# Gated mix of two attentions on one core: where the single maximum matmul stands around a step that has none

## The chip, the core and the metric

The kernel runs on one core of one Trainium2 chip. The metric is the device time of one execution in microseconds (us); lower is better. Before the change the median of three runs is 1461.88 us (1461.84 to 1462.23). A profiled execution is one more run, with the hardware profiler on.

The engines of the core have short names in the profile: PE is TensorE (matmuls; PEld is its weight loads), DVE is VectorE, ACT is ScalarE, POOL is GpSimd, SP issues DMAs.

## The reference

```python
x = A_x                                                     # (1, 2048, 512)
g = _sigmoid((x * gate_w).sum(-1, keepdims=True))
a = _A_ref(x, A_wqkv, A_wo)          # 32 heads of 16, window of 8 keys, 2 apart
b = _B_ref(x, B_wq, B_wk, B_wv, B_wo)
return g * a + (1 - g) * b

def _B_ref(x, wq, wk, wv, wo):       # 32 query heads of 16, one key/value head
    q = (x @ wq).reshape(B, S, H, Dh).transpose(0, 2, 1, 3)
    k, v = x @ wk, x @ wv
    scores = jnp.einsum("bhqd,bkd->bhqk", q, k) * (Dh ** -0.5)
    o = jnp.einsum("bhqk,bkd->bhqd", _softmax(scores, axis=-1), v)
    return o.transpose(0, 2, 1, 3).reshape(B, S, H * Dh) @ wo
```

Branch b is most of the work. Each of its 32 heads has 2048 x 2048 scores. Its softmax subtracts the true maximum of each row, so the scores are formed twice: once for the maxima, once for the exponentials.

## The kernel before

**Units and steps.** Branch b is cut into NU = 32 units: 4 blocks of 512 queries by 8 groups of 4 heads. A unit has NJ = 16 steps, one for each tile of 128 keys. There are thus 512 steps, numbered s; `u, kt = divmod(s, NJ)` gives the unit and the step in it. "Second step" below means kt = 1. Units count from 0.

**One step** is laid out by the loop at L1266. For TensorE it holds, in this order:
- the first scores (`exp_pair(s, 0)`, L575): two matmuls into the bank pair `e0` for two heads, in the two halves of the array's rows, followed on ACT by one exp of 128 x 1024 (L577);
- a pair (`fill_pair`, L388 into `pm`): two matmuls of scores for the maxima of a later unit, followed on DVE by a maximum over both (L417);
- perhaps a *single* (`fill_one`, L388 into `ps`, the bank `m1`): one such matmul, and on DVE one maximum (L428);
- the second scores (`exp_pair(s, 1)`, L575), into `e1`, with their exp;
- the weighted group (`weighted(s - 1)`, L585): the exps of the step before times the values, four matmuls into `po`.

The profile calls the banks `e0` and `e1` both `pe`. Scores may go into such a bank only when the exp of the step before has read it. After the last weighted group of a unit (in the first step of the next one) `finish_a` has DVE transpose `po` (L599); the next weighted group, in the second step, overwrites `po` and waits for that.

A step without a single is called *bare* here. The single can go out ahead of the second scores or behind them; the entry "later" at L1309 to L1312 picks the order.

**The planner.** The program that emits the kernel keeps running clocks `clk` of PE, ACT and DVE in us, and in `free` when it thinks that a bank is free. It decides with them what it emits; the chip itself waits on semaphores, not on these clocks. `single_share` (L988) adds to a stock `share`, every step, the singles still to do over the steps still to go, at most 1 a step and 2 in all. `singles` (L979) decides whether step s takes one and takes 1 from the stock. It needs a stock of 1.0, of 0.5 in the last step of a unit, or of 0.3 after a bare step (`bare[0]`). It also refuses when DVE's clock is over `BEHIND` = 1.35 ahead of PE's, unless the last step was bare or the stock is full. `fill_ready` (L1004) then emits the single only if the bank is thought free within M1S = 0.3 us of PE's clock. How many singles there are in all is what the pairs, one a step, leave over (`most`).

The first step of a unit takes none, except in the last eight units (L1316: `kt or not s or u >= NU - 8`).

**Output phases.** In the second steps of units 17 and 25 the loop first calls `out_phase`, which writes 8 and 4 rows of output blocks; that step then runs in the order first scores, single, second scores into `pm`.

Of the kernel before, what the change touches and what calls it, by code (L numbers as in the profile page):

```python
# [18 lines left out]
NJ = S // P  # L19
# [23 lines left out]
BEHIND = 1.35  # L43
FRONT = 468
LEAD, M2S, M1S, E1S, PER_ROW = 3.0, 0.5, 0.3, 0.2, 21
# [36 lines left out]
def gated_mix_kernel(ctx, tc, xt, wa, wk, wq, wo_a, wo_b, out):  # L82
# [21 lines left out]
    def home(v):  # L104

        return (v % NB, v - NB) if v < 2 * NB - 2 else ((v - NB) % (NB - 2), v - NB + 2)
# [3 lines left out]
    m1 = pp.tile([P, 512], F32, name="ps")  # L110
# [7 lines left out]
    clk = {"pe": 0.0, "act": 0.0, "dve": 0.0}  # L118
# [231 lines left out]
    def stack(u):  # L350
        qb, hg = divmod(u, NHG)
        for b in range(2):
            hi, lo = (qd[s, :, qb, 4 * hg + 2 * b:4 * hg + 2 * b + 2, :].rearrange("d c n -> d (c n)") for s in range(2))
            ap = [list(x) for x in hi.ap]
            twice = bass.AP(tensor=hi.tensor, offset=hi.offset, ap=[ap[0], [0, 2]] + ap[1:])
            dst = qst[home(u)[0]].rearrange("p c n -> p (c n)").bitcast(F32)
            nc.sync.dma_start(dst[64 * b:64 * b + 32], twice)
            nc.sync.dma_start(dst[64 * b + 32:64 * b + 48], lo)
        stacked.append(clk["pe"] + (7.5 if pe else 5.0))
# [7 lines left out]
    free = {"m2": 0.0, "m1": 0.0, "e0": 0.0, "e1": 0.0, "po": 0.0}  # L367
# [22 lines left out]
    def to_go():  # L390
        return 2 * len(slots) + len(half)
# [82 lines left out]
    def half_back():  # L474

        nc.sync.dma_start(q67.rearrange("p g x n -> p (g x n)").bitcast(F32), kd.rearrange("p g x n -> p (g x n)"))
        kcd[0] = q67
# [90 lines left out]
    pe, pexp, exped = [], {}, {}  # L568
# [174 lines left out]
    def prepare(j, n, copy=None):  # L743
        nonlocal pool
        hi, lo = turned[j, 1] = [pe[0].tile([P, C, P], F32R, name=f"own{x}", bufs=1) for x in range(2)]
        own = ob[j // 4][:, :n, j % 4 * P:(j % 4 + 1) * P]
        if copy:
            copy(hi[:, :n], own)
            at = max(clk["pe"], pool / 1e3) + 1.3
        else:  # L750
            nc.scalar.activation(hi[:, :n], own, AF.Copy)
            at = after("act", clk["pe"], 0.6)
        nc.gpsimd.tensor_sub(lo[:, :n], own, hi[:, :n].bitcast(F32))
        pool = max(pool, 1e3 * at) + 1300
# [25 lines left out]
    def blocks_out(j):  # L780

        own = p2[0].tile([P, D], F32, name="raw", bufs=1)
        for k in range(2):
            nc.vector.transpose(own[:, k * D // 2:(k + 1) * D // 2], oa[k][:, j, :])
        after("dve", 0, 0.9)
        tasks.append((clk["dve"] + 0.3, blocks_in, (j, own)))
# [180 lines left out]
    def spread_some(k):  # L967

        while (k > 0 or row_left[0] == 1) and later_rows and spread_at[0] <= clk["pe"]:
            x = next(later_rows[0], None)  # L970
            if x is None:
                later_rows.clear()
            else:
                spread_at[0] = clk["pe"] + x
                k -= 1
# [3 lines left out]
    def singles(s):  # L979

        most = to_go() - 2 * max(0, 16 * (NU - 1) - 16 - s) - PER_ROW * max(0, NJ - 4 - outs)
        need = 0.3 if bare[0] else 0.5 if (s + 1) % NJ == 0 else 1.0
        if most <= 0 or share[0] < need or not bare[0] and share[0] < 2.0 and clk["dve"] - clk["pe"] > BEHIND:
            return False
        share[0] -= 1.0
        return True

    def single_share(s):  # L988

        left = 16 * (NU - 1) - 16 - s  # L990
        if left > 0:
            most = to_go() - 2 * left - PER_ROW * max(0, NJ - 4 - outs)
            rate = most / left
            if len(stacked) < NU:
                ready = len(half) + 2 * sum(x[0] < len(stacked) for x in slots[:16 * NB])
                wait = 16 * (home(len(stacked))[1] + 1) + LAND - s
                rate = min(rate, ready / wait - 2)
            share[0] = min(2.0, share[0] + max(0.0, min(1.0, rate)))
        else:
            share[0] = 1.0  # L1000

    share, bare = [0.0], [False]

    def fill_ready(key, slack):  # L1004
        if fillable() and free[key] <= clk["pe"] + slack:
            clk["pe"] = max(clk["pe"], free[key])
            if key == "m1":
                fill_one()
            elif half and (not slots or slots[0][0] >= len(stacked) or stacked[slots[0][0]] > clk["pe"]):
                fill_one(m2[:, 0, :], "m2")  # L1010
            elif slots:
                fill_pair(m2, "m2")

    def pause(most):
        n = 0
        while n < most and slots and fillable():
            key = min(("e0", "e1", "m2"), key=lambda k: free[k])
            clk["pe"] = max(clk["pe"], free[key])
            if half:
                fill_one({"e0": eb[0], "e1": eb[1], "m2": m2}[key][:, 0, :], key)  # L1020
                n += 1
                continue
            fill_pair({"e0": eb[0], "e1": eb[1], "m2": m2}[key], key)
            n += 2
        return n
# [28 lines left out]
    def run_tasks():  # L1054
        for task in [t for t in tasks if t[0] <= clk["pe"]]:
            tasks.remove(task)
            task[1](*task[2])
# [208 lines left out]
    for s in range(NS + 1):  # L1266
        u, kt = divmod(s, NJ)
        if s == 16 * NB + 4:
            half_back()
        if len(stacked) < NU and s >= 16 * (home(len(stacked))[1] + 1):  # L1270
            stack(len(stacked))
        if s < NS and kt == 0 and u not in shifted:
            while u not in shifted:
                clk["pe"] += 0.5
                run_tasks()
                if u not in shifted and left.get(u, 1):
                    assert pause(4)
        v = min(x[0][0] for x in (half, slots, [(NU,)]) if x)
        need = left.get(v, NF // NU)
        steps = 16 * v - 6 - s  # L1280
        short = need - 2.8 * max(0, steps) if v < NU else 0
        lead = (NF - to_go()) / 64 - s / 16
        order = (0, "m2", "later") if s else ()
        rows = 4 if outs else 8
        k, n = (outs + rows) // 4 - 1, C - (outs >= NJ - 4)
        if outs == NJ - 4:
            if s in (16 * NU - 40, 16 * NU - 32):
                blocks_out(outs + (s - 16 * NU + 40) // 8)
            if to_go() <= 9 and not later_rows and "last" not in done:
                later_rows.append(spread(list(range(outs, NJ)), n))  # L1290
            if short > 0 and steps < 2:
                pause(short)
        elif due or outs < NJ and s and kt == 0 and outs // NH in done and NHG * (k + 1) - 1 in shaped and (lead < LEAD or s >= 16 * (NHG * (k + 2) + 1)):
            if not due:
                prepare(outs, n)
                due.append(n)
            else:
                out_phase(list(range(outs, outs + rows)), due.pop(), kt == 1)
                outs += rows
                order = (0, "m1", 2)  # L1300
        elif short > 0 and steps < 2:
            pause(short)

        first = 0
        some = min(4, -(-(row_prods[0] - TO_END) // (NS + 1 - s)))
        order = list(order)
        single_share(s)
        while order:
            which = order.pop(0)  # L1309
            if which == "later":  # L1310
                order = ["m1", 1] if free["e1"] > clk["pe"] - E1S else [1, "m1"]
                first = 0  # L1312
            elif which == "m2":
                fill_ready("m2", M2S)
            elif which == "m1":
                one = not later_rows and (kt or not s or u >= NU - 8) and singles(s)  # L1316
                bare[0] = not one
                if one:
                    first = half[0][4] if half else 0
                    fill_ready("m1", M1S)  # L1320
            elif s < NS:
                if which == 1:
                    spread_some(some)
                exp_pair(s, which % 2 or which // 2, which == 2, first)
        if s == NS:
            spread_some(some)
        if s:
            weighted(s - 1)
            if kt == 0 and s < NS:
                finish_a(u - 1, nc.gpsimd)  # L1330
        run_tasks()
        run_pool()
# [65 lines left out]
```

## Time and profile before

| | |
|---|---|
| median of three runs | 1461.88 us |
| the profiled execution, its own time | 1461.75 us |
| its span, first to last instruction | 1460.0 us |
| mean granted TensorE clock | 0.999 |
| projections and first maxima, until the first exp | 0 to 262.86 us |
| steps 0 to 272 | to 830.2 us |
| output phase in unit 17 | to 904.1 us |
| units 17 to 24 | to 1171.5 us |
| output phase in unit 25 | to 1210.0 us |
| units 25 to 31 | to 1448.2 us |
| the last rows | to 1460.0 us |

How to read the rows. A timeline row has the start in us, the duration in us, the engine, the line, the operation, what it writes and reads, and a count of merged instructions; in brackets stands how long the engine was idle just before, and what ended that wait. A merged row's duration covers all of its instructions. A row of the windows view has start and end of the stretch, its length, then the busy time of PE, PEld, DVE, ACT and POOL in it with the number of instructions, the granted clock, and the DMA engines' share and GB/s. Its sum row adds the lengths. A group row of the page has the shape, the count, the busy time in all, the mean of one in ns, and the engine's idle time before them with what ended it.

### The profile page before, as it was taken

The numbers are of one execution on the slowest core, as the hardware profiler recorded it, in microseconds if no ns is written. First come the engines' busy times: TensorE is split into PE (matmuls) and PEld (weight loads), VectorE is DVE, ScalarE is ACT, GpSimd is POOL, SyncE is SP. The second block draws the span as 40 slices with busy tenths as digits, with TensorE's granted clock in tenths as the row PEclk, the third lists the DMA queues.
The fourth block names the chain that finished last, engine by engine and source line by source line (L and its number), as shares of the span: only waits on it lengthen the run. The fifth ranks groups of instructions, "written<-read, shape, count | busy, mean of one in ns | idle before, by whom it ended". The sixth has DMA issues, their size and how long they took to land.

```text
span 1460.0 us, 28999 instructions
## 1 busy us (share of the span) xinstructions
PE 1450.1 (99%) x10612; PEld 674.5 (46%) x10612; DVE 1192.3 (82%) x1866; ACT 1285.6 (88%) x1627; POOL 1001.5 (69%) x1753
## 2 busy tenths in 40 slices
PE   9999999999999999999999999999999999999998
PEld 5877777433333333333333476333333363333343
DVE  6988889688888888888888888888888888888712
ACT  5659889999999999999999888999999988999986
POOL 7852889878898988988979898788888240011221
PEclk9999999999999999999999999999999999999999
DMA  6752533222021120211211111121120000000110
GB/s 226 210 165 75 148 96 101 70 57 82 27 86 42 45 90 12 72 42 42 74 46 46 60 42 62 40 71 42 42 72 12 12 27 16 12 1 2 29 32 29
DMA packets 75263, 89.80 MB, mean 62 GB/s; under 512 B 56368, under 2 KB 56416, under 8 KB 70896
## 3 DMA queue, kind: packets, MB, share of 16 engines
q1 hardware_dynamic: 68176, 49.00, 12.0%
q0 software_dynamic: 6368, 37.90, 7.8%
q8 instruction: 83, 1.36, 0.4%
q10 hardware_dynamic: 576, 1.05, 0.2%
q14 instruction: 60, 0.49, 0.1%
HBM read 60.03 MB, written 27.35 MB: 60 GB/s over the span
## 4 chain that ended last, share of the span: by engine, by line
PE 96%; DVE 2%; ACT 0%; POOL 0%; issue 0%; DVEq 0%; POOLq 0%; ACTq 0%
PE po L585 35%; PE pe L575 23%; PE pe L1213 11%; PE pm L388 8%; PE ps L388 6%; PE pe L869 4%; PE pm L484 3%; PE ps L484 2%; PE po L484 1%; PE pm L940 1%; PE pe L212 1%; DVE mx L417 1%; DVE mx L428 0%; PE po L186 0%; DVE tt L599 0%
## 5 line engine op out<-in xcount | busy, mean ns | idle before, releaser
L577 ACT ACTIVATE pexp<-pe 128x1024 f32<-128x1024 f32 x1022 | 987.1, 1022 | 83.1 <-PE pe L575 79.9
L417 DVE TENSOR_REDUCE mx<-pm 128x2 f32<-128x1024 f32 x505 | 618.0, 1224 | 144.6 <-PE pm L388 141.1
L585 PE MATMUL po<-pexp,vst 128*32 128x512 f32 x4096 | 545.5, 605 | 0.8 <-DVE tt L599 0.8
L575 PE MATMUL pe<-qst,kst 64*128 64x512 f32 x1916 | 442.2, 451 | 0.0
L575 PEld LDWEIGHTS pe<-qst,kst 64*128 64x128 f32 x1916 | 179.9, 183 | 473.5 <-ACT pexp L577 467.5
L428 DVE TENSOR_REDUCE mx<-ps 128x1 f32<-128x512 f32 x404 | 275.0, 681 | 1.9 <-PE ps L388 1.9
L388 PE MATMUL pm<-kst,qst 62*128 62x512 f32 x975 | 196.8, 397 | 0.4 <-ACT pexp L577 0.4
L649 POOL TENSOR_TENSOR pr<-aext 128x256 f32<-128x256 f32 x256 | 182.0, 738 | 2.8 <-DMA aext<-ad 2.5
L709 POOL TENSOR_TENSOR oa<-oa,av 128x256 f32<-128x256 f32 x224 | 164.1, 732 | 15.0
L585 PEld LDWEIGHTS po<-pexp,vst 128*32 128x32 f32 x4096 | 80.6, 108 | 167.6 <-issue 158.0
L388 PE MATMUL ps<-kst,qst 62*128 62x512 f32 x396 | 156.0, 394 | 0.2 <-DVE mx L428 0.2
L706 POOL TENSOR_TENSOR av<-aext,lg 128x256 f32<-128x256 f32 x224 | 139.3, 622 | 13.5
L1213 PE MATMUL pe<-wah,xh 64*128 64x512 f32 x376 | 119.3, 396 | 1.1 <-DVE stage L318 1.1
L1213 PE MATMUL pe<-wah,xl 64*128 64x512 f32 x376 | 119.7, 394 | 0.0
L1213 PE MATMUL pe<-wal,xh 64*128 64x512 f32 x376 | 118.9, 394 | 0.0
L513 ACT ACTIVATE dd<-pm 128x512 f32<-128x512 f32 x180 | 102.1, 606 | 15.2 <-PE pm L484 6.8
L388 PEld LDWEIGHTS pm<-kst,qst 62*128 62x128 f32 x975 | 94.3, 186 | 4.2 <-DVE mx L417 1.1
L655 POOL TENSOR_TENSOR tr<-pr 128x512 f32<-128x512 f32 x64 | 81.8, 1277 | 4.2
L513 ACT ACTIVATE pexp<-pm 128x512 f32<-128x512 f32 x124 | 70.5, 605 | 14.4 <-PE pm L484 7.0
L655 POOL TENSOR_TENSOR tr<-tr 128x256 f32<-128x256 f32 (+1 forms) x128 | 72.4, 566 | 8.7
L612 POOL TENSOR_TENSOR rl<-rl,gate_t 128x16 f32<-128x16 f32 x31 | 6.9, 221 | 103.6 <-DVE rl L606 96.2
L388 PEld LDWEIGHTS ps<-kst,qst 62*128 62x128 f32 x396 | 74.0, 187 | 4.3 <-issue 1.2
(215 smaller groups left out, 1965.6 us busy)
## 6 DMA issues: line engine op xcount, KB each, us to landing
aext<-ad POOLq DMA_DIRECT2D x32, 1056.0 KB, 5.5
qst<-qd SPq DMA_DIRECT2D x60, 128.0 KB
ad<-stage SPq DMA_DIRECT2D x32, 240.0 KB
xraw<-xt SPq DMA_DIRECT2D x16, 256.0 KB
qd<-qhi SPq DMA_DIRECT2D x16, 256.0 KB
qd<-qlo SPq DMA_DIRECT2D x16, 256.0 KB
qst<-qd SPq DMA_DIRECT2D x60, 64.0 KB
qst<-ml SPq DMA_DIRECT2D x216, 2.0 KB
```

The costliest lines, as they stand in the source:

```text
L388: nc.tensor.matmul(dst, qst[home(v)[0]][b:b + 62, pr, t * P:(t + 1) * P], kst[b:b + 62, kc * 512:(kc + 1) * 512], start=True, stop=True)
L417: nc.vector.tensor_reduce(m[:, :, pr, t, kc], dst, AX.X, ALU.max)
L428: nc.vector.tensor_reduce(m[:, odd, pr, t, kc:kc + 1], dst, AX.X, ALU.max)
L513: nc.scalar.activation(d[:, odd], m2[:, odd, :], AF.Abs)
L575: nc.tensor.matmul(bank[:, odd, :], kst[b:b + 64, kt * P:(kt + 1) * P], qst[home(u)[0]][b:b + 64, pr, :], start=True, stop=True)
L577: nc.scalar.activation(e, bank, AF.Exp, scale=SCALE)
L585: nc.tensor.matmul(po[32 * i:32 * i + 32, :], vst[:, kt, :], pexp[s, i // 2][:, i % 2, :], start=(kt == 0), stop=(kt == NJ - 1))
L649: nc.gpsimd.tensor_mul(pr[:, k], q, e[:, o:o + NH, AC:2 * AC])
L655: nc.gpsimd.tensor_add(nx, cur[:, :, 0:n], cur[:, :, n:2 * n])
L706: nc.gpsimd.tensor_mul(av, e[:, o:o + NH, 2 * AC:].rearrange("p j (h d) -> p j h d", d=DH), lg[:, w].unsqueeze(3).to_broadcast([P, NH, AG, ...
L709: nc.gpsimd.tensor_add(ao, ao, av)
L1213: nc.tensor.matmul(front[2 if x == last else x % 2][0][:, b, :], l[h], r[h], start=(i == 0), stop=(i == 3 * C - 1))
```

## The change

Two conditions of the planner are changed.

```diff
     def singles(s):
 
         most = to_go() - 2 * max(0, 16 * (NU - 1) - 16 - s) - PER_ROW * max(0, NJ - 4 - outs)
-        need = 0.3 if bare[0] else 0.5 if (s + 1) % NJ == 0 else 1.0
-        if most <= 0 or share[0] < need or not bare[0] and share[0] < 2.0 and clk["dve"] - clk["pe"] > BEHIND:
+        need = -0.6 if s > NJ and s % NJ == 1 else 0.3 if bare[0] else 0.5 if (s + 1) % NJ == 0 else 1.0
+        if most <= 0 or share[0] < need or not bare[0] and s % NJ != 1 and share[0] < 2.0 and clk["dve"] - clk["pe"] > BEHIND:
             return False
         share[0] -= 1.0
         return True
@@
             if which == "later":
-                order = ["m1", 1] if free["e1"] > clk["pe"] - E1S else [1, "m1"]
+                order = ["m1", 1] if free["e1"] > clk["pe"] - E1S or bare[0] and free["m1"] < clk["pe"] - 1.0 else [1, "m1"]
                 first = 0
```

Edit 1 (`singles`): from unit 1 on, the second step of a unit takes a single down to a stock of −0.6, and is not refused for DVE's lag. Edit 2 (the order at "later"): after a bare step the single also goes ahead of the second scores when its bank is thought free for more than 1 us; before, it went ahead only where the second scores' bank was thought free no earlier than E1S = 0.2 us before PE's clock.

## The prediction, written before the result was known

> **What bounds the kernel now.** I read the page first, for who is busy and which chain ends last.
>
> ```profile
> PE 1450.1 (99%) x10612; PEld 674.5 (46%) x10612; DVE 1192.3 (82%) x1866; ACT 1285.6 (88%) x1627; POOL 1001.5 (69%) x1753
> PE 96%; DVE 2%; ACT 0%; POOL 0%; issue 0%; DVEq 0%; POOLq 0%; ACTq 0%
> L577 ACT ACTIVATE pexp<-pe 128x1024 f32<-128x1024 f32 x1022 | 987.1, 1022 | 83.1 <-PE pe L575 79.9
> L428 DVE TENSOR_REDUCE mx<-ps 128x1 f32<-128x512 f32 x404 | 275.0, 681 | 1.9 <-PE ps L388 1.9
> ```
>
> TensorE is nearly the whole chain, but "busy" here includes matmuls that sit in the queue behind a wait. ScalarE at 88% is close behind: a step holds two exps. So the question is where inside a step TensorE waits, and whether the change fills that wait with work that has to be done anyway.
>
> Second, the timeline of single steps. A step is measured from the start of one weighted group (L585) to the next, since all 4096 of those records are there, 8 to a step. The first five matmul rows below are step 35 (unit 2, fourth step). It follows a step without a single and has its single **behind** the second scores. The rows from 920.62 are step 281 (unit 17, tenth step): it too follows a step without a single, but its single goes out **ahead**.
>
> ```profile
> 334.65 0.50 PE L575 MATMUL pe<-qst,kst 64*128 64x512 f32 x2
> 334.99 0.40 PE L388 MATMUL pm<-kst,qst 62*128 62x512 f32 x2
> 335.35 0.19 PEld L575 LDWEIGHTS pe<-qst,kst 64*128 64x128 f32 x2 [0.35 <-ACT pexp L577]
> 335.35 0.50 PE L575 MATMUL pe<-qst,kst 64*128 64x512 f32 x2
> 335.69 0.39 PE L388 MATMUL ps<-kst,qst 62*128 62x512 f32 x1
> 336.01 1.07 PE L585 MATMUL po<-pexp,vst 128*32 128x512 f32 x8
> ...
> 920.62 0.50 PE L575 MATMUL pe<-qst,kst 64*128 64x512 f32 x2
> 920.96 0.40 PE L388 MATMUL pm<-kst,qst 62*128 62x512 f32 x2
> 921.19 0.39 PE L388 MATMUL ps<-kst,qst 62*128 62x512 f32 x1
> 921.31 0.50 PE L575 MATMUL pe<-qst,kst 64*128 64x512 f32 x2
> 921.74 1.07 PE L585 MATMUL po<-pexp,vst 128*32 128x512 f32 x8
> ```
>
> Counted from the first scores, the second scores start at +0.70 in one and +0.69 in the other: they wait for the exp that frees their bank, whichever order is used. What differs is what comes after: behind, the single starts at +1.04 and the weighted group at +1.36; ahead, the single has run at +0.57 inside the wait and the weighted group starts at +1.12. That is 0.24 us of TensorE time for the same work.
>
> Third, the windows view, one window to a step, for all steps of four kinds. Columns: length, then busy time of PE, PEld, DVE, ACT and POOL.
>
> ```profile
> 333.66:336.01 2.35, 2.35 (x18) 0.80 (x16) 1.68 (x2) 2.35 (x3) 2.12 (x5) 1.00 0.00 0
> 1107.99:1110.34 2.35, 2.35 (x17) 0.81 (x15) 1.69 (x2) 2.35 (x4) 2.23 (x5) 1.00 0.04 7
> sum 25.90, PE 25.90 PEld 8.96 DVE 19.71 ACT 25.90 POOL 23.20; mean PE 2.35 PEld 0.81 DVE 1.79 ACT 2.35 POOL 2.11
> ...
> 302.66:304.79 2.13, 2.13 (x18) 0.87 (x16) 1.93 (x4) 2.13 (x3) 1.97 (x3) 1.00 0.00 0
> 1331.01:1333.19 2.18, 2.18 (x18) 0.82 (x16) 1.58 (x3) 2.18 (x3) 1.47 (x5) 1.00 0.00 0
> sum 108.99, PE 108.99 PEld 44.06 DVE 81.01 ACT 108.68 POOL 81.90; mean PE 2.14 PEld 0.86 DVE 1.59 ACT 2.13 POOL 1.61
> ...
> 1137.78:1139.92 2.14, 1.98 (x15) 0.64 (x15) 2.14 (x4) 1.98 (x3) 1.90 (x4) 1.00 0.33 94
> 1343.85:1345.99 2.14, 1.98 (x16) 0.65 (x15) 2.14 (x4) 1.98 (x3) 0.00 (x0) 1.00 0.00 0
> sum 10.70, PE 9.90 PEld 3.21 DVE 10.70 ACT 9.86 POOL 1.90; mean PE 1.98 PEld 0.64 DVE 2.14 ACT 1.97 POOL 0.38
> ...
> 331.76:333.66 1.90, 1.90 (x17) 0.70 (x15) 1.90 (x4) 1.90 (x4) 1.77 (x3) 1.00 0.03 9
> 1106.10:1107.99 1.89, 1.89 (x16) 0.69 (x14) 1.89 (x4) 1.69 (x3) 1.40 (x3) 1.00 0.00 0
> sum 17.17, PE 17.17 PEld 6.07 DVE 16.83 ACT 15.69 POOL 13.10; mean PE 1.91 PEld 0.67 DVE 1.87 ACT 1.74 POOL 1.46
> ```
>
> - *Behind after bare*: 11 steps, 25.90 / 11 = 2.355 us each. All steps of this kind up to unit 29.
> - *Ahead after bare*: 51 steps, 108.99 / 51 = 2.137 us.
> - *Second step without a single* in units 24, 26, 27, 28 and 29: 5 steps, 10.70 / 5 = 2.140 us.
> - *Third step without a single* after a second step that had one (units 2 to 23): 9 steps, 17.17 / 9 = 1.908 us.
>
> So a step without a single normally takes 1.91 us, one with it 2.13, a single being worth 0.23; but in the third group the step pays for a single and does none.
>
> **The change part by part.** The number of singles is fixed by what the pairs leave over (`most` in `singles` counts it down), so neither edit adds or removes a matmul or a reduce; both only move them. No DMA is moved, and SP's and POOL's queues keep their order. Which way a branch goes I take from the planner's own arithmetic over the kernel before; no time below comes from its clocks.
>
> *Edit 2, the order after a bare step (L1311).* What moves is one weight load, one matmul of 512 columns and one 681 ns reduce. The new test asks that the last step was bare and that the bank `m1` is free by over 1 us on the planner's clock. After a bare step it is 1.4 to 2.3 us free, so every single that follows a bare step now goes ahead. In 84 steps it did already; it is new in the 11 above. In units 30 and 31 no single is left, and both orders emit the same. Behind the single in TensorE's queue stand the second scores and the weighted group; a single that waited for its bank would hold both. It does not:
>
> ```profile
> 331.65 1.22 DVE L417 TENSOR_REDUCE mx<-pm 128x2 f32<-128x1024 f32 x1
> 332.78 0.68 DVE L428 TENSOR_REDUCE mx<-ps 128x1 f32<-128x512 f32 x1
> ```
>
> The second row is the last user of the bank before step 35, done at 333.46, 1.76 us before the single would go (335.22, when the pair is through). Gain: 11 × (2.355 − 2.137) = **2.40 us**; with the 0.24 of the two steps side by side it is 2.6.
>
> [...]
>
> *Edit 1, the second step of a unit (L982, L983).* In units 1 to 23 the first step has no single and the second takes one already; nothing changes there. In units 24 to 29 the first step has one, and the second is refused because DVE is 1.39 to 1.43 us ahead of TensorE on the planner's clock, over `BEHIND` = 1.35, or its share is short. Now it takes one. Unit 26:
>
> ```profile
> 1243.59 0.71 DVE L599 STREAM_TRANSPOSE tt<-po 128x512 f32<-128x512 f32 x1
> 1243.78 0.41 PE L575 MATMUL pe<-qst,kst 64*128 64x512 f32 x2
> 1244.22 1.19 DVE L417 TENSOR_REDUCE mx<-pm 128x2 f32<-128x1024 f32 x1
> 1244.35 1.06 PE L585 MATMUL po<-pexp,vst 128*32 128x512 f32 x8 [0.16 <-DVE tt L599]
> 1245.33 0.23 DVE L606 RECIPROCAL rl<-tt 128x16 f32<-128x16 f32 x1
> 1246.12 1.23 DVE L417 TENSOR_REDUCE mx<-pm 128x2 f32<-128x1024 f32 x1 [0.56 <-PE pm L388]
> ...
> 1247.81 0.40 PE L388 MATMUL pm<-kst,qst 62*128 62x512 f32 x2
> ```
>
> The weighted group waits for the transpose of the last unit's output (done 1244.30). A single behind the second scores, 0.34 after them as in step 35, would start at 1244.12 and the weighted group 0.32 later, at 1244.44; with the closer spacing of a step that does not wait, it fits wholly into the wait. I take the step as staying at 2.14, and 5 × 0.09 = 0.45 for the range. For it another step loses its single: share falls by 1, the planner's lag rises over `BEHIND`, and the third step becomes the bare one, at 1.908. Gain: 5 × (2.140 − 1.908) = **1.16 us**. The fourth step then follows a bare one and takes its single ahead, at 2.137, as the third does now.
>
> What is late next is DVE: the new reduce takes 0.68, and it has 0.56 idle before the third step's pair reduce, which so starts 0.12 later. The following pair needs that bank 0.46 after the reduce now ends (1247.81 against 1247.35), 0.23 less with the shorter step: 0.11 is left. If that cover were gone, each late tenth would cost a tenth.
>
> Unit 25's second step is its output phase:
>
> ```profile
> 1209.43 0.62 PE L575 MATMUL pm<-qst,kst 64*128 64x512 f32 x2
> 1209.73 0.69 DVE L530 CUSTOM_DVE_ANT_0 pexp<-ps,pexp 128x512 f32<-128x512 f32 x1
> ```
>
> There the planner has `m1` free 0.85 after its clock, more than the 0.3 that `fill_ready` allows, so `singles` says yes, a share is spent, and nothing goes out: 0. If it did go out, it would wait for that sum (to 1210.42) and hold the scores of 1209.43 by 1.0 + 0.23 = 1.2 us. I take 0, and 1.2 for the range.
>
> **Sum.** 2.40 + 1.16 = 3.56. The profiled execution ran 1461.75 us with a span of 1460.0; 1461.75 − 3.56 = 1458.2. The median of the runs is 0.13 above it, so 1458.3.
>
> **The rivals.**
>
> 1. *The flip gains nothing*: TensorE's saved time returns as a wait in the next step, since ScalarE is busy for all of the 2.35 (25.90 of 25.90). Against: the second scores start at +0.70 and +0.69, so ScalarE gets its work no later, and the 51 steps "ahead" cost 2.137 with ScalarE as full (108.68 of 108.99). Only edit 1 would count: 1460.7.
> 2. *The bare step stays dear*: moved from the second to the third step it costs 2.14 as now, because DVE's lag came along, or it lands beside another bare step. For: in units 24 to 29 the first step has a reduce that units 2 to 23 lack. Against: the pair reduce of the second step starts 0.13 ahead of the weighted group in unit 26 (1244.22 and 1244.35) and 0.11 ahead in unit 2 (331.65 and 331.76), where the single follows without harm. Only edit 2 would count: 1459.5.
> 3. *Slower, by DVE's queue*: the place is the second and third steps of units 24 to 29. If DVE has no idle time there, the new reduce holds the next pair's bank for all of its 0.68, and the single, not hidden, adds 0.23: 5 × 0.91 = 4.6 against 3.56, so 1462.9; if two pairs in a row are held, 5 × 1.59 = 8.0, so 1466.3. It decides once the third step's reduce starts over 0.23 later than now. For: DVE is busy for 10.70 of 10.70 in those second steps. Against: the 0.56 of idle time right behind them. [...]
> 4. *The change does nothing*: the flips alter the planner's clocks and it lays the singles out anew, with as many late steps elsewhere: 1461.9.
>
> **How the numbers follow.** The forecast, 1458.3, has 0.67; rivals 1 to 4 have 0.08, 0.11, 0.09 and 0.05. What can be told from no change here is 0.2%, 2.9 us: the lines are at 1459.0 and 1464.8. The forecast's own range is 1457.4 to 1459.5: 2.6 in place of 2.40 and a late step fewer below; 0.45 for the second steps and some of unit 25's 1.2 above. Of its 0.67 I put 0.62 below 1459.0. So faster is 0.62; same is the other 0.05, rivals 1, 2 and 4, and 0.03 of rival 3, together 0.32; slower is the 0.06 left of rival 3. The range of 8 in 10 is 1457.3 to 1460.7: it takes in rival 2, reaches rival 1, and holds unit 25's 1.2 on top of the forecast.
>
> **What would show it.** The windows of 2.35 after a bare step are gone up to unit 29, with the single at +0.57; second steps of units 24 and 26 to 29 have a `ps` matmul and still take 2.14, third steps take 1.91; TensorE's and DVE's instruction counts are the same. It is wrong if the 2.13 steps grow, if L417's idle time on `pm` is replaced by a wait of `pm` for DVE, or if as many steps of 2.35 stand elsewhere.

## The result, and the profile after

The changed kernel takes 1458.97 us in the median of 16 runs (1458.61 to 1459.97); the kernel before, run beside it, 1461.82 (16 runs, 1461.45 to 1462.29). The ratio is 0.998, with a 95% interval of 0.9974 to 0.9987. That is 2.85 us or 0.195%: a gain that is surely there, 80% of the 3.56 forecast, and a hair short of the prediction's line of 0.2% (0.998 × 1461.82 = 1458.90). The profiled execution ran 1458.94 us with a span of 1457.2, against 1461.75 and 1460.0.

The page of the changed kernel, rows as shown of before:

```profile
PE 1448.2 (99%) x10612; PEld 674.6 (46%) x10612; DVE 1191.8 (82%) x1866; ACT 1286.1 (88%) x1627; POOL 1003.4 (69%) x1753
PE 97%; DVE 1%; DMA 1%; ACT 0%; POOL 0%; issue 0%; DVEq 0%; ACTq 0%
L577 ACT ACTIVATE pexp<-pe 128x1024 f32<-128x1024 f32 x1022 | 987.2, 1022 | 80.6 <-PE pe L575 76.9
L428 DVE TENSOR_REDUCE mx<-ps 128x1 f32<-128x512 f32 x404 | 274.6, 680 | 1.9 <-PE ps L388 1.9
```

All five instruction counts stand as before, and the busy times are within 2 us of theirs: nothing was added or taken away. ScalarE's exps sit idle 2.5 us less in all (80.6 against 83.1), which is about the gain. Where did it come from? First step 35 again, on the timeline; its single now goes out ahead:

```profile
334.27 0.50 PE L575 MATMUL pe<-qst,kst 64*128 64x512 f32 x2
334.61 0.40 PE L388 MATMUL pm<-kst,qst 62*128 62x512 f32 x2
334.85 0.39 PE L388 MATMUL ps<-kst,qst 62*128 62x512 f32 x1
334.97 0.51 PE L575 MATMUL pe<-qst,kst 64*128 64x512 f32 x2
335.41 0.64 PE L585 MATMUL po<-pexp,vst 128*32 128x512 f32 x4
```

The single is at +0.58 from the first scores, the second scores still at +0.70, and the weighted group at +1.14 instead of +1.36, as forecast. Now the windows view of all 11 steps that were "behind after bare", and, behind the "...", of the step that follows each of them:

```profile
333.28:335.41 2.13, 2.13 (x17) 0.87 (x16) 1.45 (x2) 2.13 (x3) 2.00 (x4) 1.00 0.00 0
641.41:643.70 2.29, 2.29 (x17) 0.86 (x15) 1.70 (x4) 2.29 (x3) 2.13 (x6) 1.00 0.00 0
808.07:810.35 2.28, 2.28 (x18) 0.86 (x16) 2.03 (x4) 2.28 (x3) 1.86 (x4) 1.00 0.00 0
sum 23.79, PE 23.79 PEld 9.52 DVE 17.57 ACT 23.79 POOL 21.32; mean PE 2.16 PEld 0.86 DVE 1.60 ACT 2.16 POOL 1.94
...
568.50:570.77 2.27, 2.27 (x17) 0.76 (x15) 2.13 (x4) 2.22 (x3) 2.11 (x5) 1.00 0.00 0
sum 23.71, PE 23.71 PEld 8.55 DVE 20.71 ACT 22.12 POOL 21.31; mean PE 2.16 PEld 0.78 DVE 1.88 ACT 2.01 POOL 1.94
```

The same following steps in the kernel before:

```profile
569.46:571.60 2.14, 2.14 (x17) 0.83 (x16) 1.76 (x4) 1.85 (x3) 1.98 (x5) 1.00 0.00 0
sum 23.45, PE 23.45 PEld 9.15 DVE 18.57 ACT 19.73 POOL 21.05; mean PE 2.13 PEld 0.83 DVE 1.69 ACT 1.79 POOL 1.91
```

So the 11 steps went from 25.90 to 23.79, not to the 23.5 of 11 × 2.137, and the steps behind them grew from 23.45 to 23.71. The net gain is 2.11 − 0.26 = 1.85 us. Three of the 11 stand out with 2.29, 2.19 and 2.28 (units 11, 14 and 16), and two of the followers with 2.27 and 2.25 (units 9 and 23); all others are within 0.03 of 2.13.

Edit 1 shows in units 24 to 29. Of the second steps of units 24 and 26 to 29 the first row and the sum follow; behind the "..." the same for 13 bare steps of units 24 to 29. Left out are unit 25's output phase and three steps at the very end of unit 29.

```profile
1135.87:1138.00 2.13, 2.13 (x16) 0.75 (x15) 2.13 (x4) 1.97 (x3) 1.90 (x4) 1.00 0.30 92
sum 10.71, PE 10.71 PEld 3.76 DVE 10.71 ACT 9.88 POOL 1.90; mean PE 2.14 PEld 0.75 DVE 2.14 ACT 1.98 POOL 0.38
...
1138.00:1139.91 1.91, 1.91 (x16) 0.65 (x15) 1.91 (x4) 1.71 (x3) 1.12 (x3) 1.00 0.00 0
sum 24.74, PE 24.74 PEld 8.36 DVE 22.30 ACT 21.93 POOL 1.74; mean PE 1.90 PEld 0.64 DVE 1.72 ACT 1.69 POOL 0.13
```

Each second step now does a single and takes as long as before (10.71 against 10.70). Unit 26's, on the timeline, shows why: the weighted group still waits for the transpose (L599), and the single has run inside that wait. The last row is the third step's pair reduce.

```profile
1241.71 0.41 PE L575 MATMUL pe<-qst,kst 64*128 64x512 f32 x2
1241.97 0.39 PE L388 MATMUL ps<-kst,qst 62*128 62x512 f32 x1
1242.28 0.16 PEld L585 LDWEIGHTS po<-pexp,vst 128*32 128x32 f32 x8 [0.36 <-DVE tt L599]
...
1244.06 1.23 DVE L417 TENSOR_REDUCE mx<-pm 128x2 f32<-128x1024 f32 x1
```

What remains between the profiles is not the change's: 0.4 us of the 2.8 stand before the first weighted group (265.30 against 265.70), where both programs are the same. That is scatter of a single execution, as is a few tenths of each stretch below.

### The profile page after: what moved, and what is told of

Same layout as the page of the kernel before. It is cut to its first block, busy times and chain, and to the rows that moved or that the text cites. A ratio compares the mean times of both kernels' runs of the same rounds, so it can differ in the third digit from the quotient of the medians.

```text
span 1457.2 us, 28999 instructions
## 1 busy us (share of the span) xinstructions
PE 1448.2 (99%) x10612; PEld 674.6 (46%) x10612; DVE 1191.8 (82%) x1866; ACT 1286.1 (88%) x1627; POOL 1003.4 (69%) x1753
## 3 DMA queue, kind: packets, MB, share of 16 engines
q8 instruction: 83, 1.36, 0.4%
## 4 chain that ended last, share of the span: by engine, by line
PE 97%; DVE 1%; DMA 1%; ACT 0%; POOL 0%; issue 0%; DVEq 0%; ACTq 0%
PE po L585 35%; PE pe L575 24%; PE pe L1213 11%; PE pm L388 8%; PE ps L388 6%; PE pe L869 4%; PE pm L484 3%; PE ps L484 2%; PE po L484 1%; PE pm L940 1%; PE pe L212 1%; DMA xraw<-xt 1%; PE po L388 0%; PE pe L760 0%; PE po L1040 0%
## 5 line engine op out<-in xcount | busy, mean ns | idle before, releaser
L577 ACT ACTIVATE pexp<-pe 128x1024 f32<-128x1024 f32 x1022 | 987.2, 1022 | 80.6 <-PE pe L575 76.9
L417 DVE TENSOR_REDUCE mx<-pm 128x2 f32<-128x1024 f32 x505 | 618.0, 1224 | 142.7 <-PE pm L388 139.5
L585 PEld LDWEIGHTS po<-pexp,vst 128*32 128x32 f32 x4096 | 80.6, 108 | 165.2 <-issue 156.2
```

Of the source, the lines that this page charges most:

```text
L417: nc.vector.tensor_reduce(m[:, :, pr, t, kc], dst, AX.X, ALU.max)
L577: nc.scalar.activation(e, bank, AF.Exp, scale=SCALE)
L585: nc.tensor.matmul(po[32 * i:32 * i + 32, :], vst[:, kt, :], pexp[s, i // 2][:, i % 2, :], start=(kt == 0), stop=(kt == NJ - 1))
```

## The experiments

The theory after this result: the change works by one thing, a single put inside a wait that TensorE has anyway. Each edit does so by itself, and what is missing from the sum are steps that had another wait as well. There are three rivals. The steps of 2.35 may be a matter of ScalarE's pace and not of the order; the missing part may be scatter; or the bare steps may have moved to worse places.

**One edit alone.** The first kernel has edit 1 (L982, L983) on the kernel before, the second has edit 2 (L1311).

```diff
+need = -0.6 if s > NJ and s % NJ == 1 else 0.3 if bare[0] else 0.5 if (s + 1) % NJ == 0 else 1.0
+if most <= 0 or share[0] < need or not bare[0] and s % NJ != 1 and share[0] < 2.0 and clk["dve"] - clk["pe"] > BEHIND:
```

> Edit 1 alone, on the kernel before. Theory (a single put where TensorE waits anyway is free): second steps of units 24 and 26 to 29 stay at 2.14 with a single in them, the bare step that this makes elsewhere costs 1.90, and units 24 to 29 gain 0.9 us as they did with both edits: 1460.9. Rival (the bare step stays dear wherever it lands): no gain, 1461.8.

```diff
+order = ["m1", 1] if free["e1"] > clk["pe"] - E1S or bare[0] and free["m1"] < clk["pe"] - 1.0 else [1, "m1"]
```

> Edit 2 alone, on the kernel before. Theory: of the 11 moved singles those whose second scores are late gain 0.22 each; the three whose pair is late (units 11, 14, 16) gain 0.07 to 0.17, and in units 9 and 23 some 0.13 comes back in the next step, so 1.5 us in all: 1460.3. First rival (all 11 gain alike): 2.4, 1459.4. Second rival (ScalarE sets the pace and the time comes back): 1461.8.

Edit 1: 1460.64 (11 runs), 0.85 below the 1461.49 of the kernel before beside it, ratio 0.9995 (0.9987 to 1.0004). Edit 2: 1459.69 (11 runs), 1.80 below, ratio 0.9988 (0.9979 to 0.9997). They add to 2.65, nearly the 2.85 of both together. Edit 1 alone cannot be told from no change by its interval, but the trace shows the gain in the units where the edit acts. One window over units 24 to 29, first edit 1 alone:

```profile
1138.03:1376.93 238.90, 238.40 (x1733) 99.11 (x1733) 204.21 (x299) 217.26 (x253) 36.50 (x69) 1.00 0.04 12
```

and the kernel before:

```profile
1137.78:1377.53 239.75, 238.44 (x1734) 98.96 (x1733) 204.37 (x299) 217.37 (x253) 36.53 (x69) 1.00 0.04 12
```

The gain of 0.85 is 0.8 of TensorE time that stood idle (239.75 − 238.44 = 1.31 before, 0.50 now). In the kernel before it stood in five waits for a transpose: TensorE was busy for 9.90 of the 10.70 of those second steps. Edit 2 alone, windows of its 11 steps (one of the dear ones, and the sum):

```profile
641.32:643.63 2.31, 2.31 (x17) 0.87 (x16) 1.71 (x4) 2.31 (x3) 2.15 (x6) 1.00 0.00 0
sum 23.81, PE 23.81 PEld 9.51 DVE 17.61 ACT 23.81 POOL 21.28; mean PE 2.16 PEld 0.86 DVE 1.60 ACT 2.16 POOL 1.93
```

The same three steps are dear in this other execution (2.31, 2.21, 2.27), and the same two followers (2.24, 2.25). So the missing part is no scatter, and has nothing to do with edit 1.

**All singles behind.** The changed kernel with the single behind the second scores in every step:

```diff
-order = ["m1", 1] if free["e1"] > clk["pe"] - E1S or bare[0] and free["m1"] < clk["pe"] - 1.0 else [1, "m1"]
+order = [1, "m1"]
```

> The changed kernel with every single behind the second scores, after a bare step too. Some 80 singles follow a bare step. Theory (TensorE's wait for the exp is filled or not): about 0.22 each, 17 us more than the changed kernel, 1476. Rival (ScalarE's exps set the pace, the order only shifts the wait): under 2 us more, below 1461.

It took 1478.1 (2 runs), ratio to the kernel before 1.0114 (1.0095 to 1.0132): 19 us over the changed kernel. Windows of all 80 steps that have their single behind after a bare step:

```profile
303.47:305.82 2.35, 2.35 (x18) 0.87 (x16) 2.15 (x4) 2.35 (x3) 2.11 (x5) 1.00 0.00 0
...
sum 188.93, PE 188.44 PEld 64.68 DVE 153.63 ACT 188.70 POOL 151.10; mean PE 2.36 PEld 0.81 DVE 1.92 ACT 2.36 POOL 1.89
```

80 × (2.362 − 2.145) = 17 us, 2.145 being the mean of 88 ahead steps of the changed kernel. The other 2 us go with 10 more singles (387 against 377), at 0.23 each. It is the order that makes 2.36 of 2.14 for the same work after a bare step; the rival of ScalarE's pace falls.

**Every single ahead.** Here the order is turned not only after a bare step but wherever the bank is free on the planner's clock:

```diff
-order = ["m1", 1] if free["e1"] > clk["pe"] - E1S or bare[0] and free["m1"] < clk["pe"] - 1.0 else [1, "m1"]
+order = ["m1", 1] if free["e1"] > clk["pe"] - E1S or free["m1"] < clk["pe"] else [1, "m1"]
```

> The changed kernel with the single ahead of the second scores wherever the planner thinks its bank is free at all, after a step with a single too (some 250 more steps). Theory (in those steps TensorE does not wait for the exp, so there is nothing to fill, and the bank is free only just in time): between 0 and a few hundredths more a step, 1459 to 1465. Rival (ahead is better everywhere): below 1458.

It took 1466.69 (5 runs), ratio 1.0035 (1.0021 to 1.0048), 7.7 us over the changed kernel and 1.7 past the upper end expected. The waits view from the first weighted group on has a row that the changed kernel's list lacks, and the timeline one case of it:

```profile
PEld ps L388 <- DVE mx L428: 48.4, 233, 0.4
...
571.91 0.18 PEld L388 LDWEIGHTS ps<-kst,qst 62*128 62x128 f32 x1 [0.23 <-DVE mx L428]
```

The columns of the first row are total, times and longest. After a step with a single, the bank is not free in time: the single waits for the last one's reduce, 233 times, with the second scores queued behind it. 247 such steps took 2.163 on average, against 2.133 with the single behind in the changed kernel: 7.4 us in sum. So ahead is not better as such; it is better where the single itself has nothing to wait for, and that is after a bare step.

**Why some moved steps are dear: the pair's bank.** Unit 11's step of 2.29 on the changed kernel's timeline:

```profile
641.01 0.29 DVE L398 TENSOR_REDUCE ms<-mx 128x32 f32<-128x128 f32 x1
641.33 0.21 DVE L407 STREAM_TRANSPOSE mt<-ms 128x32 f32<-128x32 f32 x1
641.47 0.21 DVE L683 RECIPROCAL asum<-asum 128x16 f32<-128x16 f32 x1
641.59 1.16 DVE L417 TENSOR_REDUCE mx<-pm 128x2 f32<-128x1024 f32 x1
642.81 0.19 PEld L388 LDWEIGHTS pm<-kst,qst 62*128 62x128 f32 x2 [0.22 <-DVE mx L417]
643.15 0.39 PE L388 MATMUL ps<-kst,qst 62*128 62x512 f32 x1
643.70 1.06 PE L585 MATMUL po<-pexp,vst 128*32 128x512 f32 x8
```

In the step before, DVE had other work (the first three rows), so that step's pair reduce (L417) ends late, at 642.75. The next pair waits for that bank, and the single, whose bank is free since 640.97, 1.84 before the pair's 642.81, stands behind the pair in TensorE's queue. The kernel before had this wait too, but there the order of single and second scores made the whole step 2.35 anyway. In the changed kernel's trace ten steps have a pair that waits for this reduce, by 0.10 to 0.23, and these ten take 2.17 to 2.31. The three dear ones among the 11 moved are among them: 0.22 in unit 11, 0.11 in unit 14, 0.19 in unit 16. The test: where the planner itself sees the pair as late, by up to the 0.5 that it allows, the single's matmul goes out ahead of the pair as well; the reduces keep their order.

```diff
 elif which == "m2":
-    fill_ready("m2", M2S)
+    if bare[0] and kt and order == ["later"] and 0.0 < free["m2"] - clk["pe"] <= M2S and free["m1"] < clk["pe"] - 1.0 and fillable() and not later_rows and singles(s):
+        bare[0], order = False, [1]
+        reduce = fill_one(defer=True)
+        fill_ready("m2", M2S)
+        reduce()
+    else:
+        fill_ready("m2", M2S)
```

> The changed kernel; after a bare step, where the planner thinks the pair's bank is not free yet, the single's matmul goes out ahead of the pair as well, and the two reduces keep their order. Theory (in the late steps of units 11, 14, 16, 25, 27 and 29 TensorE waits for the pair's bank, and the single stands behind that wait): these steps fall from 2.19 to 2.31 to 2.13, about 1.0 us in all, 1458.0. Rival (the pair's later reduce holds the next pair): nothing gained, 1459.0 or more.

A miss: 1461.57 (11 runs), ratio 1.0001 (0.9992 to 1.001). The steps in which the single now goes out ahead of the pair do take 2.12 to 2.14, mostly with 2.17 to 2.19 in the step behind. Two are an exception at 2.26, in units 12 and 17, where the pair waits 0.30. But the kernel now has more singles. The groups view from the first exp on, this kernel:

```profile
L431 DVE TENSOR_REDUCE mx<-ps 128x1 f32<-128x512 f32 x390 | 265.5, 681 | 1.1 <-PE ps L388 1.1
```

and the changed kernel:

```profile
L428 DVE TENSOR_REDUCE mx<-ps 128x1 f32<-128x512 f32 x377 | 256.3, 680 | 0.5 <-PE ps L388 0.5
```

13 more singles at 0.23 are 3.0 us, about the 2.6 by which it lies over the changed kernel (2.9 when each is measured from the kernel before run beside it). They come from the output phases, which did fewer maxima two at a time. So this run measured two things. It was made again in two forms that leave the count at 377: only in the four steps where the pair is over 0.14 late, and in these and those under 0.1 late (11 steps, the condition below; the other has its first half alone). The changed kernel ran beside them.

```diff
-0.0 < free["m2"] - clk["pe"] <= M2S
+(0.14 < free["m2"] - clk["pe"] or 0.0 < free["m2"] - clk["pe"] < 0.1) and free["m2"] - clk["pe"] <= M2S
```

> As e4, but only where the planner thinks the pair's bank over 0.14 late: four steps (units 11, 14, 16, 29) that take 2.29, 2.19, 2.28 and 2.31 in the changed kernel. The output phases meet the same maxima as in the changed kernel, so the number of singles stays at 377. Theory: these four fall to 2.13, the step behind each costs 0.05 more as in e4, 0.4 us gained on the changed kernel beside it. Rival (the late pair is paid for anyway): nothing gained.

> As e8, and also where the planner thinks the bank 0 to 0.1 late (eleven steps in all, the further ones 2.17 to 2.26 in the changed kernel); 377 singles. Theory: 0.5 us gained on the changed kernel beside it, and below both kernels. Rival: nothing gained.

> The changed kernel once more, on the same chip as the two above, as their measure: 2.85 us below the kernel before, as at first.

Four steps: 1458.41 (11 runs), ratio 0.9977 (0.9968 to 0.9986). Eleven: 1458.28 (10 runs, 1457.94 to 1458.62), ratio 0.9976 (0.9966 to 0.9985). The changed kernel: 1458.84 (11 runs, 1458.47 to 1459.57), ratio 0.998 (0.9972 to 0.9989). Each ratio is to the kernel before; the intervals overlap, so the 0.56 between the last two rests on these runs, made side by side, where 8 of the 10 runs with eleven steps are below every run of the changed kernel, and on the steps. Windows of ten of those steps, and behind the "..." of the steps that follow them, in the kernel with eleven:

```profile
352.08:354.20 2.12, 2.12 (x17) 0.87 (x15) 1.35 (x3) 2.12 (x3) 1.96 (x4) 1.00 0.00 0
sum 21.26, PE 21.26 PEld 8.38 DVE 14.45 ACT 21.26 POOL 15.74; mean PE 2.13 PEld 0.84 DVE 1.44 ACT 2.13 POOL 1.57
...
sum 21.53, PE 21.53 PEld 8.59 DVE 20.86 ACT 20.19 POOL 17.30; mean PE 2.15 PEld 0.86 DVE 2.09 ACT 2.02 POOL 1.73
```

and in the changed kernel:

```profile
352.08:354.26 2.18, 2.18 (x17) 0.82 (x15) 1.58 (x3) 2.18 (x3) 2.02 (x5) 1.00 0.00 0
sum 22.37, PE 22.37 PEld 8.38 DVE 16.73 ACT 22.37 POOL 16.65; mean PE 2.24 PEld 0.84 DVE 1.67 ACT 2.24 POOL 1.66
...
sum 21.29, PE 21.29 PEld 8.29 DVE 18.60 ACT 18.99 POOL 16.38; mean PE 2.13 PEld 0.83 DVE 1.86 ACT 1.90 POOL 1.64
```

The steps gain 1.11, and 0.24 is given back behind them. One of the followers is now a bare one, so some 0.2 more is given back, and 0.6 to 0.7 is left. The whole kernel's 0.56 holds other things as well: one late exp of the kind told in the last section is gone (three in its waits view, 1.0 us in sum, against four and 1.4), and unit 13's third step takes 0.13 more. Unit 11's step, in the kernel with four, shows how: the single at +0.34 from the first scores, the late pair behind it, the weighted group again at +1.14.

```profile
642.37 0.50 PE L582 MATMUL pe<-qst,kst 64*128 64x512 f32 x2
642.71 0.40 PE L388 MATMUL ps<-kst,qst 62*128 62x512 f32 x1
642.79 0.55 PE L388 MATMUL pm<-kst,qst 62*128 62x512 f32 x2
643.13 0.45 PE L582 MATMUL pe<-qst,kst 64*128 64x512 f32 x2
```

So the wait for the pair's bank is why these steps were dear: with the single ahead of it they take 2.12 to 2.14, and the kernel 1458.28, below the changed kernel and below the 1461.77 of the kernel before.

**Why two followers grew: branch a's exp.** In units 9 and 23 ScalarE does the small exp of branch a (L679, 0.31 us) within the moved step. With the step 0.22 shorter, the second scores of the step behind it wait 0.31 and 0.29 for ScalarE (at 570.10 and 1109.89 in the changed kernel), where 0.16 is seen in the same place behind step 35 (at 336.87). Two kernels leave out that exp, on the changed kernel and on the kernel before; the planner still counts it, and branch a's weights lack their exponential.

```diff
-nc.scalar.activation(lgv, lgv, AF.Exp, scale=SCALE)
 after("act", 0, 0.4)
```

> The changed kernel without branch a's 32 exps on ScalarE (L679, 0.31 us each); the planner still counts them, so the order of all else is the same. Branch a's weights are thus left without their exp. Theory (the 2.25 to 2.27 steps after the moved single in units 9 and 23 are ScalarE still late by that exp): they fall to 2.13, and with the third step of unit 18 and one of unit 11 about 0.4 us is gained, 1458.5. Rival (they come from something else): they stay.

> The same left out of the kernel before. Theory: the steps of 2.35 with the single behind the second scores stay as they are in at least the six units without that exp close by (7, 11 twice, 13, 14 twice, 16, 22), since there a bare step is just shorter than two exps or the pair is late; in units 2, 9 and 23 the 2.35 may fall to 2.13. At most 0.7 us gained beside what the other steps gain in the run above. Rival (branch a's exp is what makes all of them late): all 11 fall, 2.4 us gained.

On the changed kernel: 1458.08 (9 runs), ratio 0.9976 (0.9966 to 0.9986), 3.56 below its kernel before, so some 0.6 to 0.7 below the changed kernel. Windows of this kernel, the step behind the moved one in unit 9, and the corresponding one in unit 23:

```profile
568.30:570.42 2.12, 2.12 (x17) 0.77 (x15) 1.96 (x4) 1.92 (x3) 1.96 (x5) 1.00 0.00 0
1107.72:1110.12 2.40, 2.40 (x18) 0.76 (x16) 2.08 (x3) 2.40 (x3) 2.24 (x6) 1.00 0.01 3
```

Unit 9 came out as expected (2.27 to 2.12), unit 23 did not (2.25 to 2.40). There another thing, an exp that starts after 0.23 of idle time at 1107.46, now falls into the step before (see the last section). So one of the two is shown, the other only argued. On the kernel before: 1461.06 (10 runs), ratio 0.9996 (0.9986 to 1.0005), and its 11 "behind" steps stay as they were:

```profile
sum 25.85, PE 25.85 PEld 8.93 DVE 19.64 ACT 25.62 POOL 23.25; mean PE 2.35 PEld 0.81 DVE 1.79 ACT 2.33 POOL 2.11
```

Leaving out the exp gains about 0.6 us in both kernels. How much of it hangs on late exps that move is not shown: the step of unit 22 told in the last section, 2.39 and 2.40 with branch a's exp, takes 2.12 in both kernels without it, and the 2.40 above is new. Branch a's exp isn't what made the 11 steps late: the order is.

## Why the prediction came out as it did

**Edit 2, the mechanism: right.** All 11 steps turned, the single went into the wait for the exp at +0.58, the second scores stayed at +0.70. Rival 1 (nothing gained, ScalarE sets the pace) is excluded by the 17 us over 80 steps and by the 1.80 that edit 2 gains alone. Rival 4 (as many late steps elsewhere) is excluded too: one single behind a bare step is left, in unit 25 just after the output phase, 2.76 before and 2.77 after. It is not among the prediction's 11, and makes its "every single that follows a bare step now goes ahead" wrong by one. Its 51 steps "ahead after bare" are not all either: the trace of before has 77, with the same mean of 2.137.

**Edit 2, the size: this is the step that failed.** "Gain: 11 × (2.355 − 2.137) = 2.40" took step 35 for all 11 and gave each the mean of 51 others. It came to 1.80 alone and 1.85 in the windows. Three of the 11 had a second wait, the pair's for a late reduce: 0.16 + 0.06 + 0.15 over 2.13, 0.37 in sum. In two, 0.13 and 0.12 came back in the next step, shown to be branch a's exp for the first and argued for the second; over all followers it is 0.26. The term should have been 2.40 − 0.28 − 0.26 = 1.86, where 0.28 is the 23.79 less 11 × 2.137. The trace of before showed the late pairs; this is unit 11, in the very step:

```profile
643.77 0.19 PEld L388 LDWEIGHTS pm<-kst,qst 62*128 62x128 f32 x2 [0.23 <-DVE mx L417]
```

The prediction looked at what the *single* would wait for and at who stands behind it, but not at who stands ahead of it.

**Edit 1, the second step: right.** "I take the step as staying at 2.14": 2.13 to 2.15, with a single. Unit 25's yes without a single behind it also was as said: its output phase took 38.52 us against 38.50.

**Edit 1, where the bare step goes: wrong, and nearly without cost.** "The third step becomes the bare one, at 1.908" holds for unit 24 alone. In units 26 to 29 the third step takes a single too; by the planner's own arithmetic, which no trace shows, DVE is 1.33 ahead there, just under the 1.35 of `BEHIND`. The bare step comes later in the unit, and there it does cost 1.90 (13 of them in 24.74), which is all that the sum needed. That the price held although the place did not was in part luck. So rival 2 was half right about the place and wrong about the price. The gain was 0.85 to 0.9 instead of 1.16. Two of the new places have a late pair behind them, 2.20 in unit 27 (2.13 before) and 2.31 in unit 29 (2.20 before), which is 0.18 of the 0.3 missing; the rest is not traced.

**What is late next.** DVE was to start the third step's pair reduce 0.12 later; it started 1.78 behind the weighted group's start (1244.06 and 1242.28) where it had been 1.77 (1246.12 and 1244.35). In all five units it started at 1.77 or 1.78, so rival 3, which hung on a start over 0.23 later, is excluded.

**The sum.** The median of 1458.97 lies within the forecast's range of 1457.4 to 1459.5, and 0.67 above the 1458.3 itself. By the line of 0.2% it falls, by 0.07 us, on the side of "same", which had 0.32, and not of "faster", which had 0.62. The gain came to 2.85 against 3.56: 0.6 of the 0.7 missing is edit 2's size, 0.3 edit 1's, and the two together did 0.2 better than their single runs add to, which is within what executions differ by. The worth of one single held (a step goes from 1.90 to 2.13 with it, against the prediction's 0.23); what was off is the count of singles that were wholly hidden.

## What to carry to other kernels

TensorE took its matmuls here in the order of the program: unit 11's single, its bank free since 640.97, went out at 643.15, behind the pair that waited until 642.81. So put an instruction that is ready ahead of the one that waits, not behind it (0.22 in each of 80 steps here); but check *both* neighbours: that what is moved forward has nothing to wait for (233 waits and 7.7 us in the run with every single ahead), and that nothing ahead of it waits already (some 0.6 us left in ten steps). Where an edit hits several places, look up the releaser of each wait in each place, and don't multiply the nicest one: 3 of 11 had another wait, and 2 gave over half of the gain back in the next step. And where a planner shares out work, count the work afterwards before reading a time: a small edit that is right can lose 3 us to 13 singles more elsewhere.

## What was not expected

**The count of singles hangs on small things.** How many maxima an output phase does two at a time depends on where the stock of places stands when it begins. Putting the single ahead of the pair in some 16 steps made 13 more singles (3.0 us), taking them all behind made 10 more, taking them all ahead 4 more, though none of these edits touches the output phases.

**An exp that starts late without a late input.** Three steps of the changed kernel, in units 3, 22 and 28, took 2.39 to 2.42, and the same three took 2.40 in the kernel before. The step ahead of the one in unit 3 on the timeline:

```profile
376.93 3.79 ACT L577 ACTIVATE pexp<-pe 128x1024 f32<-128x1024 f32 x4 [0.23 <-PE pm L388]
```

Its scores began at 376.05, 0.88 earlier, where 0.60 is usual (1241.74 after 1241.14 in unit 26). The trace names the *pair's* matmul (376.38) as what released it, which writes another bank. Both traces have four such exps, with 1.4 us of idle time ahead of them in all: in the changed kernel 0.23, 0.47 and 0.48 at these three steps and 0.24 at one in unit 0.

Leaving out branch a's exp, with the order of all else the same, moves some of them. On the changed kernel the step in unit 3 then takes 2.14 and the one in unit 22 2.12, while in unit 23 the exp at 1107.46, in the step ahead of the 2.40 above, starts after 0.23 of idle time. The pairs stand in the same places there, so the pair's matmul alone does not make an exp late; what does is not shown. The four stand in the same steps before and after the change, with 1.4 us in all both times, so its 2.85 us hold none of it.
